# Four attention layers on one core: first row maxima in nine groups of six, normalisation on ScalarE in two layers, a projection dealt into attention's first phases

## The chip, the core and the metric

The kernel runs on one core of a Trainium2 chip. The metric is the device time in microseconds, the median of several runs. Before the change it is 5493.16 us (three runs, 5492.14 to 5493.9).

## What is computed

Four residual layers over x, 2048 tokens of 576 values in fp32: A, B, A, B. Each layer normalises x, projects it, does softmax attention with 32 heads of 18 values, projects the result back and adds it to x. In layers A every head has its own keys and values; in layers B all heads share one key and one value head.

```python
def _A_ref(x, wqkv, wo):                       # H = 32, Dh = 18
    q, k, v = split_heads(x @ wqkv)
    p = softmax(einsum("bhqd,bhkd->bhqk", q, k) * Dh ** -0.5)
    return merge(einsum("bhqk,bhkd->bhqd", p, v)) @ wo
...
x = x + _A_ref(layernorm(x), A_wqkv, A_wo)
x = x + _B_ref(layernorm(x), B_wq, B_wk, B_wv, B_wo)   # as A, one k and one v head for all
x = x + _A_ref(layernorm(x), A_wqkv, A_wo)
x = x + _B_ref(layernorm(x), B_wq, B_wk, B_wv, B_wo)
```

## The kernel before

**Number format.** Values that go through a projection are split into a high and a low part in TensorE's fp32r format; a projection of 512 tokens onto 128 columns is 14 matmuls (`TERMS`, line 32). Queries and keys stand in `big` with three rows for each value of a head (high, low, high against high, high, low), and two more rows that carry the negated row maximum, so that one matmul gives the score minus the maximum.

**A layer.** Layers are numbered 0 to 3; 0 and 2 are A (`is_a`), 1 and 3 are B. A layer has four stretches.

1. The previous layer's output projection (`out_proj`, `out_w`, lines 365 and 432), 16 chunks of 128 tokens. Between them the first chunks of x are normalised (`stats`, `scaled`, lines 301 and 313) and transposed by TensorE (`trans`, line 391). `stats` is VectorE and two small GpSimd instructions; `scaled` is two VectorE instructions.
2. The projections (loop at line 795), token block T of 512 by column tile t, with the transposes of the following chunks between them (`advance`, line 418). `project` (line 470) does the 14 matmuls into one PSUM bank, then evicts: high part by ScalarE (line 490), low part by VectorE (line 496) or, for a `filler`, by a second ScalarE copy and a GpSimd subtraction (lines 493 and 494). `store` sends the parts to a DRAM scratch, and `load_k` and `load_q` bring the rows of a head pair back into `big`. All these transfers are issued by SyncE, whose queue is in order. In layers B the order of t is 4, 0, 1, 2, 3; tile 4 holds the keys and values. In layers A values have projections of their own (`natural`, line 265, 14 matmuls of 288 columns).
3. A fill (lines 839 to 849 and 1024 to 1030): projections that the first head pair does not need.
4. Attention (lines 1038 to 1051): 16 head pairs by 4 blocks of 512 queries, 64 units of 32 exponentials (`exp_mm`, line 870: one score matmul and one ScalarE exponential of 128x512) and 32 maxima (`max_mm`, line 623: one score matmul and one VectorE reduction of 128x512). `UNIT` (lines 70 to 79) is the order, written by hand, of one unit in ten phases: e is an exponential, m a maximum, r a maximum whose block is first brought to SBUF by a ReLU on ScalarE (line 650) and then combined with its partner in one VectorE instruction (line 655), the digits are the head of the pair and the place in the list of banks. Each phase ends with so many columns of value matmuls (`pv_cols`), which lag 832 columns behind (`PV_LAG`), so that the first phase has none and the second none either.

**The first maxima.** The maxima run 56 ahead of the exponentials (`LEAD` = 14 steps of four). The first 56 are therefore put among the projections: `woven` (line 292) calls `max_pairs` (line 718), four maxima, after every so many matmuls that call `beat` (line 284). In layers A that is 8 calls 13 matmuls apart in the last value projections, then 6 calls 7 apart (lines 1025 and 1026); in layers B 5 calls 10 apart in block T = 2, 6 calls 6 or 7 apart in T = 3 and 3 in the fill (lines 804 to 807 and 1028). `max_place` and `m_first` (lines 592 and 611) say which query block and key block each is.

When all 32 maxima of a unit are there, `max_final` (line 851) reduces them, `max_store` (line 859) sends them to DRAM and `max_rows` (line 865) brings them back as rows of `big`; the exponentials of that unit wait for that. `todo` (line 968) holds such steps by the exponential at which they are due: `max_store`, `max_rows`, the loads of later pairs (`load_part`), the differences of keys for r (`diff_in` to `diff_rows`, lines 677 to 716), the output steps `o_mul` and `o_out` (lines 954 and 958).

**PSUM and spare buffers.** Seven banks are handed out oldest first (`bank`, `aged`, lines 158 to 164); a projection holds one until it ends. `relu` (line 966) is the list of buffers for the ReLU: one tile and, during attention, the chunk of x named in `AWAY` (line 65), which `x_away` (line 973) copies to DRAM at the start of attention and `x_back` returns near its end.

## Time and profile before

| what | value |
|---|---|
| median of three runs | 5493.16 us |
| profiled execution | 5495.69 us, span 5493.8 us |
| TensorE (PE) busy | 5479.3 us, 100%, 68190 matmuls |
| VectorE (DVE) busy | 4944.7 us, 90% |
| ScalarE (ACT) busy | 4810.0 us, 88% |
| GpSimd (POOL) busy | 1052.3 us, 19% |

PE is TensorE's matmuls and PEld its weight loads, which overlap them; DVE, ACT, POOL and SP are VectorE, ScalarE, GpSimd and SyncE, a q behind a name is that engine's queue. Matmuls are pipelined, so their durations overlap and the distance from start to start says what one costs. L877 is line 877 of the kernel before: the exponentials' score matmuls; L652 are the maxima's, L481 the projections, L275 the value projections, L927 the value matmuls; L882 is the exponential and L657 the maximum's reduction. In a row of the timeline the first number is the start in us of the span, the second the duration, and what stands in brackets is the engine's idle time before it and what ended it. xN says that the row merges N instructions.

### The profile page before, as it was taken

To read this page: it belongs to the slowest core of one execution; us is meant where nothing else is said; L and a number is where in the kernel's file an instruction comes from. 1 tells how busy PE (TensorE), PEld (TensorE's weight loads), DVE (VectorE), ACT (ScalarE), POOL (GpSimd) and SP (SyncE) were. 2 spreads that over 40 slices of the span, in tenths; PEclk is the share of its full clock that TensorE was granted. 3 is DMA by queue.
4 is the path that set the end of the run, shared out by engine and by line. 5 is a ranking of instruction groups with operands and counts; after the bars stand their busy time and mean duration, and the time that the engine had idled before them with its cause. 6 is when DMAs were issued, how large, how long until landed. Compare 5 with 4: busy or idle time off the path is not lost.

```text
span 5493.8 us, 166922 instructions
## 1 busy us (share of the span) xinstructions
PE 5479.3 (100%) x68190; PEld 3441.6 (63%) x68190; DVE 4944.7 (90%) x9741; ACT 4810.0 (88%) x9634; POOL 1052.3 (19%) x1614
## 2 busy tenths in 40 slices
PE   9999999999999999999999999999999999999999
PEld 8655555555855555555786555555558555555557
DVE  4799999998799999999637999999977999999995
ACT  3599999999289999999626999999992999999996
POOL 3121111212212111111211211111122121111111
PEclk9999999999999999999999999999999999999999
DMA  6321111111421110101253211111114111110102
GB/s 220 120 64 46 51 47 52 46 49 38 136 60 35 28 28 25 28 25 29 67 176 109 64 52 47 48 50 50 44 48 133 56 32 28 28 28 25 28 19 87
DMA packets 304321, 322.21 MB, mean 59 GB/s; under 512 B 130290, under 2 KB 239434, under 8 KB 294266
## 3 DMA queue, kind: packets, MB, share of 16 engines
...
## 4 chain that ended last, share of the span: by engine, by line
PE 97%; DMA 1%; DVE 1%; SPq 1%; POOL 0%; issue 0%; ACT 0%; POOLq 0%; ACTq 0%; DVEq 0%
PE oacc L927 38%; PE pse L877 23%; PE psm L652 21%; PE psn L275 7%; PE psq L481 6%; PE psm L639 2%; DVE mx L657 1%; PE ps L261 0%; POOL ev L494 0%; DMA m_d<-tr 0%; DMA big<-m_d 0%; DMA xx<-qk_d 0%; DMA rb<-r_d 0%; PE oacc L262 0%; SPq L553 0%
## 5 line engine op out<-in xcount | busy, mean ns | idle before, releaser
L882 ACT ACTIVATE pt<-pse 128x512 f32<-128x512 f32 x8192 | 4228.1, 613 | 62.1 <-PE psm L652 5.5
L657 DVE TENSOR_REDUCE mx<-psm 128x1 f32<-128x512 f32 x6208 | 3906.3, 683 | 113.0 <-PE psm L652 94.7
L652 PE MATMUL psm<-big 62*128 62x512 f32 x7200 | 2361.3, 438 | 1.9 <-ACT xo L650 1.1
L877 PE MATMUL pse<-big 64*128 64x512 f32 x8192 | 2358.5, 437 | 4.0 <-DMA big<-m_d 2.9
L927 PE MATMUL oacc<-pt,vbuf 128*19 128x256 f32 (+5 forms) x34864 | 1710.2, 319 | 0.1
L877 PEld LDWEIGHTS pse<-big 64*128 64x128 f32 x8192 | 1180.2, 184 | 478.8 <-ACT pt L882 167.0
L652 PEld LDWEIGHTS psm<-big 62*128 62x128 f32 x7200 | 1165.9, 184 | 445.9 <-ACT pt L882 342.1
L927 PEld LDWEIGHTS oacc<-pt,vbuf 128*19 128x19 f32 x34864 | 779.6, 98 | 733.2 <-issue 429.4
L943 POOL TENSOR_TENSOR rl<-lt,mone 128x8 f32<-128x8 f32 x256 | 419.6, 1639 | 1043.3 <-DMA lt<-os 1042.9
L927 PE MATMUL oacc<-pt,vy 128*19 128x256 f32 (+2 forms) x12272 | 570.5, 311 | 0.0
L186 POOL TENSOR_SCALAR hl<-neg 128x8 fp32r<-128x8 f32 x256 | 50.7, 198 | 2418.4 <-DVE neg L853 2418.4
L927 PEld LDWEIGHTS oacc<-pt,vy 128*19 128x19 f32 x12272 | 277.7, 98 | 250.7 <-issue 165.1
L490 ACT ACTIVATE ev<-psq 128x512 fp32r<-128x512 f32 (+1 forms) x112 | 66.9, 597 | 310.8 <-PE psq L481 224.3
L655 DVE CUSTOM_DVE_ANT_0 xo<-psm,xo 128x512 f32<-128x512 f32 x496 | 337.0, 679 | 0.8 <-PE psm L652 0.8
L655 DVE CUSTOM_DVE_ANT_0 relu<-psm,relu 128x512 f32<-128x512 f32 x496 | 337.2, 680 | 0.0
L650 ACT ACTIVATE xo<-psm 128x512 f32<-128x512 f32 x496 | 317.2, 640 | 1.5 <-DMA x_d<-xo 1.5
L275 PE MATMUL psn<-wsm,xx 128*128 128x288 f32 x2240 | 310.1, 297 | 0.0
L275 PEld LDWEIGHTS psn<-wsm,xx 128*128 128x128 f32 x2240 | 298.9, 188 | 12.1 <-issue 9.7
L650 ACT ACTIVATE relu<-psm 128x512 f32<-128x512 f32 x496 | 297.5, 600 | 0.0
L496 DVE TENSOR_TENSOR ev<-psq,ev 128x512 fp32r<-128x512 f32 (+1 forms) x84 | 57.9, 691 | 205.7 <-ACT ev L490 189.8
L956 POOL TENSOR_TENSOR os<-os,rb 128x256 f32<-128x256 f32 x256 | 188.1, 735 | 151.1 <-DMA rb<-r_d 96.6
L639 PE MATMUL psm<-big 54*128 54x512 f32 x512 | 204.9, 400 | 0.1
...
## 6 DMA issues: line engine op xcount, KB each, us to landing
...
rb<-r_d SPq DMA_DIRECT2D x512, 64.0 KB
...
o_d<-os SPq DMA_DIRECT2D x1024, 18.0 KB
...
big<-m_d SPq DMA_DIRECT2D x512, 4.0 KB
```

Source lines behind the costliest of these rows:

```text
L275: nc.tensor.matmul(ps, lhs[:, xc, :], wsm[:, wc, h * 288:(h + 1) * 288], start=i == 0, stop=i == len(TERMS) - 1)
L481: nc.tensor.matmul(ps[:n].rearrange("p (u t) -> p u t", u=2)[:, us], w[:, wc, :n], xts[T][:, us, xc, :], start=(xc, wc) == TERMS[0], stop= ...
L639: nc.tensor.matmul(ps.rearrange("p (h t) -> p h t", h=2) if p == 0 or not is_a else ps, q[b:b + 3 * DH, c0:c0 + P], k, start=True, stop=True)
L650: nc.scalar.activation(t, ps, AF.Relu)
L652: nc.tensor.matmul(ps, q[b:b + KM, c0:c0 + P], k[b:b + KM, kb * 512:(kb + 1) * 512], start=True, stop=True)
L655: nc.vector.tensor_tensor_reduce(t, ps, t, 1.0, LOWEST, OP.add, OP.max, mx[:, r:r + 1])
L657: nc.vector.reduce_max(mx[:, r:r + 1], ps, axis=AX.X)
L877: nc.tensor.matmul(e, k[r:r + KE, kc * P:(kc + 1) * P], q[r:r + KE, u * 512:(u + 1) * 512], start=True, stop=True)
L882: nc.scalar.activation(pt, e, AF.Exp, scale=SCALE)
L927: nc.tensor.matmul(oacc[j:j + DH + 1, c0:c1], v_of(kc)[:, 2 * p + a if is_a else 0, :], pts[tiles[a]][:, 256 * h + c0:256 * h + c1], start ...
L943: nc.gpsimd.tensor_tensor(rl, lts.pop((p, u)), mone, op=OP.pow)
L956: nc.gpsimd.tensor_tensor(t, t, rb, op=OP.mult)
```

## The change

- The first maxima are nine groups of six (`max_group`), called at written places (`A_AT`, `B_AT`) counted in matmuls: in layers A from ahead of the value projections on, in layers B from block T = 1 on; the last two are issued just before attention. `M_FIRST` says which they are. The first unit's `max_store` and `max_rows` and one load of queries are called at places too.
- In layers B `scaled` is two ScalarE instructions (Identity with scale and bias), for which `stats` gets a third GpSimd instruction; the evictions are of the filler kind from T = 1 on; the last block's keys and values are projected ahead of three of block 2's queries, and the transposes are drawn forward for that.
- The fill's last projection (column tile 3 of block 3) is not run in the fill. Its 14 matmuls are taken from a generator: up to eight ahead of the fifth operation of the first phase and the rest in the second, while it holds its bank; its eviction follows the last one.
- In layers A the last block's tile 4 comes before tile 0, and some loads move.
- Two chunks of x are away during attention instead of one (`AWAY`), so there are three buffers for the ReLU; they are copied away in block T = 3. There are three tiles for the later maxima instead of two. `o_mul` writes to the other half of its tile. The differences for the second pair start four steps later.

```diff
-AWAY = (15,)
+AWAY = (14, 15)
+A_AT = (88, 112, 126, 146, 166, 196, 220, 246, 268)
+B_AT = (28, 48, 68, 90, 106, 122, 142, 154, 178)
+M_FIRST = (((0, 0, 0, 4), (0, 1, 0, 4), (0, 2, 0, 4), (1, 0, 0, 3), (0, 3, 0, 4), (1, 0, 3, 4), (1, 1, 0, 4),
+            (1, 2, 0, 4), (1, 3, 0, 4)),
+           ((0, 0, 0, 4), (0, 1, 0, 4), (1, 0, 0, 4), (0, 2, 0, 4), (1, 1, 0, 2), (0, 3, 0, 4), (1, 1, 2, 4),
+            (1, 2, 0, 4), (1, 3, 0, 4)))
...
+LATE = 8
...
-    mx2 = [cst.tile([P, 32], F32, name=f"mx{i}") for i in range(2)]
+    mx2 = [cst.tile([P, 32], F32, name=f"mx{i}") for i in range(MX)]
...
+    def ranked(rank):
+        return [i for i in lru if i not in held][rank]
+
     def oldest(rank=0):
 
-        return lambda name: bank(lru[rank], name)
+        return lambda name: bank(ranked(rank), name)
...
-    weave = {"left": 0}
+    weave = {"n": 0, "at": []}
 
     def beat():
-        if weave["left"]:
-            weave["n"] += 1
-            if weave["n"] == weave["every"]:
-                weave["n"] = 0
-                weave["left"] -= 1
-                weave["f"]()
-
-    def woven(f, left, every):
-        assert not weave["left"]
-        weave.update(f=f, left=left, every=every, n=0)
+        weave["n"] += 1
+        while weave["at"] and weave["n"] >= weave["at"][0][0]:
+            weave["at"].pop(0)[1]()
+
+    def woven(*places):
+        assert not weave["at"]
+        weave.update(n=0, at=sorted(places, key=lambda x: x[0]))
...
-        rs = pool.tile([P, 2], F32, bufs=4, name="rs")
+        rs = pool.tile([P, 3], F32, bufs=4, name="rs")
...
         nc.gpsimd.tensor_tensor(rs[:, 1:2], rs[:, 0:1], mhalf, op=OP.pow)
+        if layer % 2:
+            nc.gpsimd.tensor_scalar(rs[:, 2:3], mv[:, 0:1], -1.0, rs[:, 1:2], op0=OP.mult, op1=OP.mult)
...
     def scaled(c, mv, rs):
         xc = xo[:, c, :]
         xh = pool.tile([P, 640], F32, tag="xh", bufs=2, name="xh")
-        nc.vector.tensor_scalar(xh[:, :D], xc, mv[:, 0:1], rs[:, 1:2], op0=OP.subtract, op1=OP.mult)
-        nc.vector.tensor_scalar(xh[:, D:], xc[:, 512:], mv[:, 0:1], rs[:, 1:2], op0=OP.subtract, op1=OP.mult)
+        if layer % 2:
+            nc.scalar.activation(xh[:, :D], xc, AF.Identity, bias=rs[:, 2:3], scale=rs[:, 1:2])
+            nc.scalar.activation(xh[:, D:], xc[:, 512:], AF.Identity, bias=rs[:, 2:3], scale=rs[:, 1:2])
+        else:
+            nc.vector.tensor_scalar(xh[:, :D], xc, mv[:, 0:1], rs[:, 1:2], op0=OP.subtract, op1=OP.mult)
+            nc.vector.tensor_scalar(xh[:, D:], xc[:, 512:], mv[:, 0:1], rs[:, 1:2], op0=OP.subtract, op1=OP.mult)
         return xh
...
-        def project(T, t, filler=False, half=None, terms=TERMS):
+        def project(*args, **kw):
+            for _ in project_parts(*args, **kw):
+                beat()
+
+        def project_parts(T, t, filler=False, half=None, terms=TERMS):
             t0 = T * 512
...
             for xc, wc in terms:
                 nc.tensor.matmul(ps[:n].rearrange("p (u t) -> p u t", u=2)[:, us], w[:, wc, :n], xts[T][:, us, xc, :],
                                  start=(xc, wc) == TERMS[0], stop=(xc, wc) == (TERMS if half != 0 else TERMS_LO)[-1])
-                beat()
+                yield
...
-        m_first = [] if is_a else ([(0, i // 2, i % 2) for i in range(8)] + [(1, i // 2, i % 2) for i in range(4)] +
...
+        m_first = [(u, i, kb) for u, kb, n, n1 in M_FIRST[layer % 2] for i in range(n, n1)]
...
-            if i < len(m_first):
+            if i < 32:
                 return (0, *m_first[i])
...
-                mxs[p, u] = pool.tile([P, 32], F32, name="mx") if (p, u) < (0, 2) else mx2[u % 2]
+                mxs[p, u] = pool.tile([P, 32], F32, name="mx") if (p, u) < (0, 2) else mx2[(4 * p + u) % MX]
...
-        def max_pairs():
-
-            if is_a:
-                if m_done[0] == 40:
-                    load_q(0, 1024, S)
-                run_todo(m_done[0] // 4)
-            elif m_done[0] == 44:
-                max_store(0, 0)
-            elif m_done[0] == 48:
-                max_rows(0, 0)
-            for i in range(4):
+        def max_group():
+            for i in range(6):
                 max_mm()
             while m_full:
                 max_final(*m_full.pop()[0])
...
+        def x_away():
+            for i, c in enumerate(AWAY):
+                nc.sync.dma_start(x_d[i], xo[:, c, :])
...
-        rest = [1, 2, 3, 5] if is_a else [2, 3]
+        rest = [1, 2, 5, 3] if is_a else [2, 3]
+        order = []
         for T in range(4):
-            if T == 0 and not is_a:
-                fixed_rows(k_slot(0), True)
-                fixed_rows(q_slot(0), False)
             if is_a:
-                ts = range(0 if T or layer else 3, 9) if T < 3 else (6, 7, 8, 0, 4)
+                ts = range(0 if T or layer else 3, 9) if T < 3 else (6, 7, 8, 4, 0)
             else:
                 ts = (4, 0, 1, 2, 3) if T < 3 else (4, 0, 1)
-            for i, t in enumerate(ts):
-                if not is_a and T == 2 and i == 1:
-                    woven(max_pairs, 5, 10)
-                elif not is_a and T == 3:
-                    woven(max_pairs, 2, (7, 6, 7)[i])
-                project(T, t, not is_a and T >= 2)
+            order += [(T, i, t) for i, t in enumerate(ts)]
+        if not is_a:
+            order.insert(12, order.pop(15))
+        for T, i, t in order:
+                if T == 0 and i == 0 and not is_a:
+                    fixed_rows(k_slot(0), True)
+                    fixed_rows(q_slot(0), False)
+                if not is_a and T == 1 and i == 0:
+                    woven(*((n, max_group) for n in B_AT), (B_AT[7] + 6, lambda: max_store(0, 0)),
+                          (B_AT[7] + 16, lambda: max_rows(0, 0)), (B_AT[7] + 26, lambda: load_q(0, 1536, S)))
+                project(T, t, not is_a and T >= 1)
                 if is_a and T == 3 and i == 2:
                     load_k(0, 0, 1536)
-                    load_q(0, 0, 512)
+                    load_q(0, 0, 1024)
+                    diff_rows(0)
+                    woven(*((n, max_group) for n in A_AT), (A_AT[6] + 4, lambda: max_store(0, 0)),
+                          (A_AT[6] + 18, lambda: max_rows(0, 0)), (A_AT[6] + 30, lambda: load_q(0, 1024, S)))
                     last_values()
+                if is_a and T == 3 and i == 4:
+                    load_k(0, 1536, S)
+                if T == 3 and i == (3 if is_a else 1):
+                    x_away()
 
                 for at_i, f in ((0, diff_in), (4 if is_a else 2, diff_split), (6 if is_a else 3, diff_out)):
                     if T == 2 and i == at_i:
                         f(0)
 
-                if T < 3 and ((i in (0, 1, 3, 5) if T + layer == 0 else i % 2) if is_a else i < 4):
-                    advance()
+                if T < 3 and ((i in (0, 1, 3, 5) if T + layer == 0 else i % 2) if is_a else i < (4, 5, 2)[T]):
+                    advance(2 if not is_a and T == 2 and i == 0 else 1)
                 if T == 0 and is_a and i < 6:
                     finish_loads()
                     if layer == 0 and i < 2:
@@ -826,16 +850,16 @@
                         load_wsm(i, A_wqkv[:, 2 * D:])
                     if layer == 0 and i < 3:
                         load_x(5 + i)
-                if not is_a and i < 2:
+                if not is_a and i < 2 and T * i < 3:
                     (load_q if i else load_k)(0, T * 512, T * 512 + 512)
-                if T == 3 and i == 2:
+                if not is_a and T == 3 and i == 2:
                     diff_rows(0)
                 if vts and i != 0:
                     v_trans(*vts.pop())
-            if is_a and T < 2:
-                for c in range(4 * T, 4 * T + 4):
-                    for h in range(2):
-                        nc.scalar.activation(v_dst(c)[:, h], project_v(c, h), AF.Copy)
+                if is_a and T < 2 and t == 8:
+                    for c in range(4 * T, 4 * T + 4):
+                        for h in range(2):
+                            nc.scalar.activation(v_dst(c)[:, h], project_v(c, h), AF.Copy)
         fill = []
         if is_a:
             for c in range(12, NCH):
@@ -844,10 +868,6 @@
         for t in rest:
             fill.append((project, (3, t, True)))
 
-        if is_a:
-            load_k(0, 1536, S)
-            load_q(0, 512, 1024)
...
             a, kc = (i // 2) % 2, i // 4 * 2 + i % 2
             q, k = ops(p)
-            by_act = reader[lru[rank]]
+            by_act = reader[ranked(rank)]
             e = oldest(rank)("pse")
...
         def o_mul(p, u):
-            t = sums[u % 2][:, :256]
-            nc.gpsimd.tensor_tensor(t, t, rb, op=OP.mult)
+            t = sums[u % 2]
+            nc.gpsimd.tensor_tensor(t[:, 256:], t[:, :256], rb, op=OP.mult)
 
         def o_out(p, u):
             for a in range(2):
                 c = (2 * p + a) * DH
                 for h in range(2):
                     j, t0 = 64 * a + 32 * h, u * 512 + 256 * h
-                    nc.sync.dma_start(o_d[c:c + DH, t0:t0 + 256], sums[u % 2][j:j + DH, :256])
+                    nc.sync.dma_start(o_d[c:c + DH, t0:t0 + 256], sums[u % 2][j:j + DH, 256:])
...
-        def x_away():
-            for i, c in enumerate(AWAY):
-                nc.sync.dma_start(x_d[i], xo[:, c, :])
-
         def x_back():
             for i, c in enumerate(AWAY):
                 nc.sync.dma_start(xo[:, c, :], x_d[i])
 
-        at(LEAD, x_away)
...
-                if is_a or p or u:
+                if p or u:
                     at(b + NM_AT, max_store, p, u)
                     at(b + (SOON[2] if b == ns - 1 else ROW_AT), max_rows, p, u)
...
                 for d, f in ((0, diff_in), (3, diff_split), (5, diff_out), (10 if p else 8, diff_rows)):
-                    at(max(LEAD, 32 * p - 8) + d, f, p + 1)
+                    at(max(LEAD + 4, 32 * p - 8) + d, f, p + 1)
...
+        late = project_parts(*fill.pop()[1])
         for i, (f, args) in enumerate(fill):
-            if is_a and i % 8 == 0:
-                woven(max_pairs, *((8, 13), (6, 7))[i // 8])
-            elif not is_a and i == 0:
-                woven(max_pairs, 3, 6)
             f(*args)
-        assert not weave["left"] and m_done[0] == 4 * LEAD
+        assert not weave["at"], weave
+        while m_done[0] < 4 * LEAD:
+            max_mm()
         e_next = [0, 0]
 
         def exp_next(a, rank=0, first=False):
@@ -1040,6 +1054,9 @@
             rows, cols = UNIT[phase % len(UNIT)]
             run_todo(LEAD + sum(e_next) / 4)
             for i, (kind, a, rank) in enumerate(rows):
+                if i == 4 and lagged < PV_LAG:
+                    for _ in range(LATE):
+                        next(late, None)
                 if kind == "e":
```

## Rows read from the trace of the kernel before

**Rows 1.** The page, busy time and share of the span of each engine.
```profile
PE 5479.3 (100%) x68190; PEld 3441.6 (63%) x68190; DVE 4944.7 (90%) x9741; ACT 4810.0 (88%) x9634; POOL 1052.3 (19%) x1614
```

**Rows 2.** Windows: PE, PEld, DVE, ACT, POOL busy, granted clock, DMA share, GB/s.
```profile
400.00:1340.00 940.00, 940.00 (x12767) 555.11 (x12755) 919.68 (x1802) 928.48 (x1853) 189.04 (x282) 1.00 0.17 46
1435.00:1475.00 40.00, 40.00 (x199) 32.27 (x198) 28.92 (x70) 12.63 (x28) 6.88 (x17) 1.00 0.58 191
1525.00:1535.00 10.00, 9.74 (x86) 4.93 (x83) 8.21 (x16) 8.32 (x17) 1.68 (x3) 0.83 0.75 237
```

**Rows 3.** Groups of instructions by line, 400 to 1340 us, the exponentials.
```profile
L882 ACT ACTIVATE pt<-pse 128x512 f32<-128x512 f32 x1648 | 851.5, 609 | 11.5
```

**Rows 4.** Timeline of PE in steady attention, layer 0.
```profile
1001.52 0.78 PE L877 MATMUL pse<-big 64*128 64x512 f32 x3
...
1002.31 0.90 PE L927 MATMUL oacc<-pt,vbuf 128*19 128x160 f32 x16
```

**Rows 5.** The chain of waits in layer 0: start, us, what.
```profile
146.32 14.83 PE psn L275 x112
...
172.50 1.92 PE psn L275 x13
175.08 1.93 PE psn L275 x13
```

**Rows 6.** Timeline of layer 1, projections and the start of attention.
```profile
1448.92 0.58 DVE L316 TENSOR_SCALAR xh<-xo,mv,rs 128x576 f32<-128x576 f32 x1
...
1482.11 1.66 PE L481 MATMUL psq<-yx,big 128*128 128x512 f32 x6 [0.47 <-DVE mx L657]
...
1487.47 1.34 PE L652 MATMUL psm<-big 62*128 62x512 f32 x4
...
1509.37 1.33 PE L652 MATMUL psm<-big 62*128 62x512 f32 x4
...
1512.46 0.73 PE L652 MATMUL psm<-big 62*128 62x512 f32 x4
...
1516.44 7.22 DVE L657 TENSOR_REDUCE mx<-psm 128x1 f32<-128x512 f32 x12
...
1516.97 1.27 PE L652 MATMUL psm<-big 62*128 62x512 f32 x4
...
1519.75 1.49 PE L652 MATMUL psm<-big 62*128 62x512 f32 x4
...
1524.37 0.47 PE L877 MATMUL pse<-big 64*128 64x512 f32 x1 [0.18 <-DMA big<-m_d]
...
1531.46 0.60 ACT L882 ACTIVATE pt<-pse 128x512 f32<-128x512 f32 x1 [1.53 <-PE psm L652]
```

**Rows 7.** Timeline of layer 0, last projection and the start of attention.
```profile
203.88 3.48 PE L481 MATMUL psq<-xx,big 128*128 128x512 f32 x14
...
207.29 0.50 PE L877 MATMUL pse<-big 64*128 64x512 f32 x1
...
207.63 0.40 PE L652 MATMUL psm<-big 62*128 62x512 f32 x2
...
207.86 0.39 PE L877 MATMUL pse<-big 64*128 64x512 f32 x1
...
208.43 4.53 ACT L882 ACTIVATE pt<-pse 128x512 f32<-128x512 f32 x9
...
212.05 0.95 PE L927 MATMUL oacc<-pt,vbuf 128*19 128x256 f32 x16
...
226.77 0.47 PE L877 MATMUL pse<-big 64*128 64x512 f32 x1 [0.57 <-DMA big<-m_d]
...
227.28 0.60 ACT L882 ACTIVATE pt<-pse 128x512 f32<-128x512 f32 x1 [0.89 <-PE psm L652]
```

**Rows 8.** Waits of ACT, 2940 to 3050 us, layer 2: total, times, longest.
```profile
ACT pt L882 <- PE psm L652: 1.6, 2, 0.9
```

**Rows 9.** Timeline of layer 3, the start of attention, ACT.
```profile
4272.22 0.60 ACT L650 ACTIVATE xo<-psm 128x512 f32<-128x512 f32 x1 [1.47 <-DMA x_d<-xo]
```

40 lines of the change are left out of this document (21 added, 19 removed).

## The prediction, made before the changed kernel was run

> **What bounds the kernel now.** The page comes first: TensorE is busy all the span, VectorE 90%, ScalarE 88% [rows 1]. A busy TensorE need not be full, so the windows come next: in a long stretch of layer 0's attention all three are nearly full (940.00, 919.68 and 928.48 of 940 us [rows 2]). That stretch holds 1648 exponentials [rows 3], so a unit of 32 exponentials and 32 maxima takes 940 × 32 / 1648 = 18.25 us. Which engine sets it shows in TensorE's own timeline: trains of score matmuls at 1001.52, then the value matmuls at 1002.31, each starting where the one before lets it, with no idle time noted [rows 4]. So attention is bound by TensorE, and the waits of ScalarE and VectorE follow it.
>
> Ahead of a layer's attention come the projections, with the first 56 maxima woven in. The chain of waits runs through TensorE there too: 112 value projections take 14.83 us, 0.132 each, and with four maxima after every 13 the period is 2.58 us (172.50 to 175.08) [rows 5]. 13 × 0.132 is 1.72, so a group of four maxima costs 0.86 us of TensorE. In layers 1 and 3 it is not full: several groups last 1.27 to 1.49 us where others take 0.73 [rows 6]. Then come the first phases: layer 0's first exponential matmul is at 207.29, the first value matmuls at 212.05, and between them ScalarE does nine exponentials in 4.53 us [rows 7]. There, and only there, TensorE has time left, because no value matmuls run for the first 832 columns.
>
> The sum is made on the profiled execution (5495.69 us around its span of 5493.8). The runs' median, 5493.16, is 2.5 us below; the same difference is taken off it. About 0.2%, 11 us, is what a measurement of this kernel can tell from no change.
>
> **The change part by part.**
>
> *Groups of six.* Fourteen groups of four become nine of six and two maxima that ride in the attention's first train. Six need one pair more than four. Pairs follow each other after 0.34 us (207.29 to 207.63) at the start of a train and after 0.23 (207.63 to 207.86) inside one [rows 7], so a group of six costs 0.86 + 0.23 = 1.09, at most 1.20. Before 14 × 0.86 = 12.0; after 9 × 1.09 + 0.23 = 10.0. That is -2.0 us a layer, -8.0 in all (-4 with 0.34 for the added pair).
>
> *The last projection.* Its 14 matmuls take 203.88 to 207.29, 3.41 us [rows 7], and leave the stretch ahead of attention. They come back as eight before the fifth operation of the first phase and six in the second, ahead of any value matmul. The blocks cost 3.41 plus one more way in and out, some 3.6 us. Around them stand 13 score matmuls of two phases and six of the third, ten pairs at 0.23 to 0.34: 2.3 to 3.4. Together 5.9 to 7.0 before the value matmuls, where it is 4.76 now: 1.2 to 2.2 longer. ScalarE also gets the block's two copies among the exponentials (0.6 each by the nearest row, an exponential), of which none may be hidden, and at worst all 3.6 is added. I take the middle of 1.2 and 3.6, 2.4. The move is worth -3.4 + 2.4 = -1.0 a layer, -4.0 in all. The 14 matmuls' result is written out by two more transfers on SyncE's queue in the first phases; their heads are not read before pair 10, and only the transfers behind them could feel it.
>
> *Waits ahead of attention in layers 1 and 3.* TensorE waits on VectorE for a free bank, or on the keys: groups of 1.34, 1.33, 1.27 and 1.49 instead of 0.73 are 0.61 + 0.60 + 0.54 + 0.76 = 2.5 us, a projection waits 0.47 and the first exponential 0.18, for the row of maxima [rows 6]: 3.2. I take 2.7 of it, as a wait of the 0.47 kind can stay. The maxima now begin one token block earlier, 20 or so matmuls apart, and the last block's keys are projected before three of the queries. Six maxima keep VectorE 6 × 0.60 = 3.6 us (12 in 7.22 [rows 6]). In the next 20 matmuls, some 4.6 us, TensorE has a transpose as well, and VectorE its parts of it; the move of the normalisation to ScalarE (0.58 us a chunk for the large piece [rows 6]) and of the evictions to ScalarE and GpSimd relieves VectorE, which is at 28.92 of 40 us in these projections while ScalarE is at 12.63 [rows 2]. So the added ScalarE work is costed at nothing, hidden by TensorE; were it not, each chunk would cost its 0.6. The same holds for a third small GpSimd instruction a chunk, with GpSimd at 6.88 of 40 [rows 2]. -2.7 a layer, -5.4 in all, none of it sure.
>
> *New waits there.* The last chunk's transposes now come right ahead of the projection that reads them: TensorE waits for ScalarE's copy, one instruction of 0.6 us. The row of maxima of the first unit is stored early enough, but its reload stands on SyncE's queue behind an eviction's store and two 288 KB copies of x; from there to the first exponential are 26 matmuls and a group, some 7 us, against 4.6 us (1519.75 to 1524.37) that store and reload take now. I take +0.6 + 0.5 = 1.1 a layer, +2.2 (0 to 6).
>
> *Starts of attention.* In layer 0 the second unit's row of maxima lands late: TensorE waits 0.57 and ScalarE 0.89 [rows 7]. Layer 2 has two such waits, 1.6 us [rows 8]. In layer 3 ScalarE waits 1.47 us to write into x's spare chunk, which is still being copied away [rows 9]. The change copies it away during the projections, and puts the second pair's differences four steps later, behind the second unit's store. I take 0.9 in layer 0, half of layer 2's 1.6 (one of its waits lies later), and 1.5 in layer 3: -3.2, none of it sure.
>
> *The clock.* Layer 1 has a wait of 1.53 at that place too [rows 6]. In the window 1525 to 1535 TensorE's granted clock was 0.83 on the mean [rows 2], so part of it at 1.2 instead of 2.4 GHz; ahead of it TensorE had been working, with no idle time in these rows beyond 0.18 and 0.47 us [rows 6]. The Trainium skill (TensorE: Matmul & The Clock Gate, "Why this matters for your kernels") puts such falls down to idle gaps between bursts of matmuls. The rows show no gap of note, so here the trace does not agree. By the page, the matmuls dealt into the first phases keep the clock up and all 1.5 us go; by the row, a fall may come anyway and none does. I take 0.7: -0.7.
>
> *The rest* is costed at nothing: the third spare buffer for the pre-maxima and the third tile of maxima act in steady attention, where TensorE is the bound; the product goes to the other half of its tile on GpSimd, which is at 19% [rows 1]; and more time between that and VectorE's next copy can only help. The second chunk of x comes back eight steps before the end, and is added to only at the output projection's fifteenth chunk.
>
> Sum: -8.0 - 4.0 - 5.4 + 2.2 - 3.2 - 0.7 = -19.1, so 5493.2 - 19.1 = **5474 us**.
>
> **The rivals.** *A transfer gates the first exponentials.* If the row of maxima, or the last keys, come as late in layers 1 and 3 as now, the 5.4 stay, and so may the 3.2 and the 0.7 at the starts: 5474 + 9.3 = 5483. For it speaks that SyncE's queue is in order and now takes x's copies before the reload; against it, 7 us of cover for 4.6.
>
> *The dealt projection is not hidden.* If the first phases grow by all 3.6 us, and six maxima in a row cost 1.20 a group, 1.2 × 4 and 4 come back: 5474 + 8.8 = 5483. For it: TensorE needs nearly all of these 4.76 us once two switches are added. Against: ScalarE's 4.53 us for nine exponentials runs beside.
>
> *The change misses: VectorE becomes the bound ahead of attention in layers 1 and 3.* Six maxima need 3.6 us, a chunk's transpose and statistics some 2 us more; in the next 20 matmuls, 4.6 us, with a group (1.1) and a transpose (0.9) that is 5.6 of 6.6, so VectorE is short only where two chunks fall into one such stretch, by about 1 us, in perhaps three places a layer: 5474 + 6 = 5480.
>
> *Slower: steady attention loses its pattern.* Four pre-maxima a unit now turn over three buffers, so the choice of the exponential's buffers, which follows who read what last, no longer repeats from unit to unit. A matmul that gets one more wait costs what a broken train costs, 0.34 - 0.23 = 0.11 us. Once a unit in 252 units is 28 us: 5474 + 28 = 5502; it decides from 0.08 a unit, where the 19 are gone. Against it: ScalarE and VectorE show slack in the window [rows 2], and TensorE's trains show no idle time [rows 4].
>
> **How the numbers follow.** The forecast's own case gets 0.58, the three mild rivals together 0.32, the slower one 0.10. Over 0.2% faster is below 5482: 0.56 of the first case and 0.10 of the mild ones, 0.66; same 0.26, of which 0.02 is the first case's and 0.02 a lesser form of the slower one; slower 0.08. Low end: the late projection at 1.2 instead of 2.4 (-4.8), no new waits (-2.2), the whole of the clock and of layer 2's waits (-1.6), and as much again in steady attention if the third buffer spares a wait somewhere: 5461. High end: past the mild rivals at 5483, to where two of them meet, 5491.
>
> **What would show it.** Right: in layers 0 and 2 the stretch from the last value projections to the first exponential shrinks by about 5.4 us, in layers 1 and 3 by some 7; the time from there to the first value matmuls grows from 4.8 to about 7; groups of six last some 1.1 us from start to start of what stands around them; ScalarE's waits of 0.9 to 1.5 us at the starts are gone; and a unit of steady attention stays at 18.25 us. Wrong: a unit of another length, as 0.04 us there are 10 us in all; a first value matmul over 8.4 us after the first exponential; waits of TensorE on VectorE around the groups; or a reload of the maxima landing after the last projection.

## The result and the profile after the change

The changed kernel takes 5519.16 us (median of four runs, 5518.48 to 5523.91), the kernel before 5492.93 beside it: the ratio is 1.005, with an interval of 1.0032 to 1.0067. The change makes the kernel 26 us slower; 5474 had been forecast, with a range up to 5491. The profiled execution is the slowest of the four, 5523.91 us around a span of 5522.1, against 5495.69 around 5493.8 before.

The page's first part and a window of steady attention, to be laid beside [rows 1, 2], and the exponentials of that window beside [rows 3]:

```profile
PE 5480.8 (99%) x68190; PEld 3451.3 (63%) x68190; DVE 4918.1 (89%) x9667; ACT 4850.5 (88%) x9708; POOL 1077.8 (20%) x1657
```

```profile
400.00:1340.00 940.00, 940.00 (x12772) 555.61 (x12772) 919.58 (x1802) 928.76 (x1855) 186.39 (x279) 1.00 0.17 47
```

```profile
L902 ACT ACTIVATE pt<-pse 128x512 f32<-128x512 f32 x1649 | 851.6, 609 | 11.2
```

TensorE has the same 68190 matmuls and 1.5 us more busy time, but the span is 28.3 us longer: TensorE stands idle for 41 us of it, where it was 14.5 before [rows 1]. Steady attention has not changed: 1649 exponentials in 940 us where there were 1648. (L902 is the exponential now, L671 and L658 the maxima, L897 the exponentials' score matmuls, L500 the projections, L287 the value projections, L947 the value matmuls, L273 and L274 the transposes.)

So the loss lies at the two ends of each layer. The table is worked out from the starts and ends of the exponentials in both traces: *front* is the time from the last exponential of the layer before (in layer 0 from the start) to the first of this layer; the first, second and third unit are 32 exponentials each, from start to start; then the last 128 exponentials, to their end. It is after less before, in us.

| layer | front | first unit | second and third | last 128 |
|---|---|---|---|---|
| 0 | +3.8 | +4.1 | +4.8 | +0.9 |
| 1 | -2.6 | +5.0 | 0.0 | +0.5 |
| 2 | +0.6 | +4.5 | +3.8 | +0.8 |
| 3 | -1.2 | +5.0 | 0.0 | +0.5 |
| sum | +0.5 | +18.6 | +8.7 | +2.6 |

Together 30.4 us; the units between and the end of the kernel give 2.1 back, which makes the 28.3 by which the spans differ. The fronts, from which 24.8 us were to go, gave nothing. Four views show the waits. The timeline of TensorE in layer 0, where the value projections begin:

```profile
151.77 5.85 PE L287 MATMUL psn<-wsm,yx 128*128 128x288 f32 x43
161.29 0.47 PE L671 MATMUL psm<-big 62*128 62x512 f32 x1 [3.67 <-DMA big<-qk_d]
162.38 1.62 PE L671 MATMUL psm<-big 62*128 62x512 f32 x5 [0.63 <-DMA big<-qk_d]
163.93 5.73 PE L287 MATMUL psn<-wsm,yx 128*128 128x288 f32 x24
```

and the window behind that wait (columns as in [rows 2], the granted clock third from the end):

```profile
162.00:169.00 7.00, 6.62 (x26) 5.93 (x27) 3.57 (x6) 0.41 (x1) 0.00 (x0) 0.52 0.01 2
```

The first group of six comes 88 matmuls after the keys' loads were issued, and the loads have not landed: TensorE waits 3.67 and 0.63 us. Behind the wait the granted clock is 0.52, so 1.2 instead of 2.4 GHz nearly throughout: 24 value matmuls take 5.73 us, where at 0.132 each [rows 5] they would take 3.17.

The same engine at the start of layer 0's third unit, and SyncE's queue ahead of it (start, us, what):

```profile
256.24 0.47 PE L897 MATMUL pse<-big 64*128 64x512 f32 x1 [2.90 <-DMA big<-m_d]
```

```profile
243.35 3.29 SPq L707 DMA_DIRECT2D xx<-qk_d x4
246.74 0.57 SPq L883 DMA_DIRECT2D m_d<-tr x1
...
247.99 2.57 SPq L735 DMA_DIRECT2D xx<-kd_d x2
...
251.70 0.52 SPq L887 DMA_DIRECT2D big<-m_d x2
```

The third unit's row of maxima (store 246.74, reload 251.70) now stands between the differences' transfers, which hold the queue for 3.29 and 2.57 us. TensorE waits 2.90 us.

Layer 1, block 2, where two chunks' transposes now come in a row:

```profile
1494.59 0.60 PE L273 MATMUL ps<-ident,xh 128*128 128x128 f32 x4
...
1495.13 0.60 PE L273 MATMUL ps<-ident,xh 128*128 128x128 f32 x4
1498.21 0.33 PE L274 MATMUL oacc<-ident,xh 128*128 128x128 f32 x1 [2.48 <-DVE xx L268]
```

The fifth transpose of a chunk goes to `oacc`, one bank for all chunks, and the second chunk's waits 2.48 us until VectorE has read the first's.

And layer 1's first phases, TensorE and ScalarE:

```profile
1535.64 0.50 PE L671 MATMUL psm<-big 62*128 62x512 f32 x2 [0.56 <-ACT evr L512]
1536.08 2.11 PE L500 MATMUL psq<-xx,big 128*128 128x512 f32 x8
...
1539.81 0.50 PE L671 MATMUL psm<-big 62*128 62x512 f32 x1 [0.73 <-ACT pt L902]
1540.24 1.66 PE L500 MATMUL psq<-xx,big 128*128 128x512 f32 x6
...
1543.13 0.50 PE L658 MATMUL psm<-big 54*128 54x512 f32 x1 [0.33 <-ACT evr L512]
...
1544.06 0.95 PE L947 MATMUL oacc<-pt,vbuf 128*19 128x256 f32 x16
```

```profile
1535.48 0.60 ACT L902 ACTIVATE pt<-pse 128x512 f32<-128x512 f32 x1
1538.68 2.06 ACT L902 ACTIVATE pt<-pse 128x512 f32<-128x512 f32 x4 [2.60 <-PE pse L897]
1542.00 0.60 ACT L509 ACTIVATE ev<-psq 128x512 fp32r<-128x512 f32 x1 [1.26 <-PE psq L500]
```

The dealt matmuls (L500, 8 and 6) stand in TensorE's queue when ScalarE has been given one exponential: it is idle for 2.60 us behind the first block and 1.26 behind the second, and then TensorE waits 0.73 for ScalarE. So no exponential runs beside the blocks. The first value matmuls come 8.58 us after the first exponential, where it was 3.62 to 4.01 in the trace before; "over 8.4" was one of the prediction's signs of being wrong.

One more wait is new in layers 1 and 3, ahead of the second unit: its row of maxima is late (the same timeline of TensorE, layer 1; in layer 3 it is 1.09).

```profile
1559.43 0.47 PE L897 MATMUL pse<-big 64*128 64x512 f32 x1 [1.28 <-DMA big<-m_d]
```

### The profile page after: what moved, and what is told of

The parts are those of the page before. It is cut to its first block, busy times and chain, and to the rows that moved or that the text cites. A ratio compares the mean times of both kernels' runs of the same rounds, so it can differ in the third digit from the quotient of the medians.

```text
span 5522.1 us, 166476 instructions
## 1 busy us (share of the span) xinstructions
PE 5480.8 (99%) x68190; PEld 3451.3 (63%) x68190; DVE 4918.1 (89%) x9667; ACT 4850.5 (88%) x9708; POOL 1077.8 (20%) x1657
## 4 chain that ended last, share of the span: by engine, by line
PE 96%; DMA 1%; DVE 1%; issue 0%; SPq 0%; ACT 0%; POOL 0%; ACTq 0%; POOLq 0%; DVEq 0%
PE oacc L947 38%; PE pse L897 23%; PE psm L671 21%; PE psn L287 6%; PE psq L500 6%; PE psm L658 2%; DVE mx L676 1%; DMA m_d<-tr 0%; PE ps L273 0%; DMA big<-qk_d 0%; DMA big<-m_d 0%; POOL ev L513 0%; ACT evr L512 0%; PE oacc L274 0%; DVE yx L267 0%
## 5 line engine op out<-in xcount | busy, mean ns | idle before, releaser
L902 ACT ACTIVATE pt<-pse 128x512 f32<-128x512 f32 x8192 | 4226.4, 611 | 82.0 <-PE pse L897 15.3
L671 PE MATMUL psm<-big 62*128 62x512 f32 x7200 | 2360.5, 438 | 13.1 <-DMA big<-qk_d 7.8
L897 PE MATMUL pse<-big 64*128 64x512 f32 x8192 | 2355.2, 437 | 8.5 <-DMA big<-m_d 8.5
L947 PE MATMUL oacc<-pt,vbuf 128*19 128x256 f32 (+5 forms) x34864 | 1709.4, 319 | 0.4 <-DVE os L198 0.3
L897 PEld LDWEIGHTS pse<-big 64*128 64x128 f32 x8192 | 1180.6, 184 | 482.3 <-ACT pt L902 174.3
L671 PEld LDWEIGHTS psm<-big 62*128 62x128 f32 x7200 | 1169.4, 184 | 456.3 <-ACT pt L902 346.4
L947 PEld LDWEIGHTS oacc<-pt,vbuf 128*19 128x19 f32 x34864 | 779.2, 98 | 731.7 <-issue 426.5
L947 PE MATMUL oacc<-pt,vy 128*19 128x256 f32 (+2 forms) x12272 | 572.1, 312 | 0.0
L674 DVE CUSTOM_DVE_ANT_0 xo<-psm,xo 128x512 f32<-128x512 f32 x664 | 452.2, 681 | 0.0
L947 PEld LDWEIGHTS oacc<-pt,vy 128*19 128x19 f32 x12272 | 278.2, 98 | 251.2 <-issue 165.8
L669 ACT ACTIVATE xo<-psm 128x512 f32<-128x512 f32 x664 | 409.6, 617 | 0.0
L287 PE MATMUL psn<-wsm,xx 128*128 128x288 f32 x2240 | 308.7, 297 | 0.0
L287 PEld LDWEIGHTS psn<-wsm,xx 128*128 128x128 f32 x2240 | 298.8, 188 | 9.9 <-issue 7.2
L674 DVE CUSTOM_DVE_ANT_0 relu<-psm,relu 128x512 f32<-128x512 f32 x328 | 223.4, 681 | 0.0
L658 PE MATMUL psm<-big 54*128 54x512 f32 x512 | 203.5, 397 | 1.2 <-ACT evr L512 1.2
L669 ACT ACTIVATE relu<-psm 128x512 f32<-128x512 f32 x328 | 202.2, 616 | 0.0
```

The source lines that it names most:

```text
L287: nc.tensor.matmul(ps, lhs[:, xc, :], wsm[:, wc, h * 288:(h + 1) * 288], start=i == 0, stop=i == len(TERMS) - 1)
L658: nc.tensor.matmul(ps.rearrange("p (h t) -> p h t", h=2) if p == 0 or not is_a else ps, q[b:b + 3 * DH, c0:c0 + P], k, start=True, stop=True)
L669: nc.scalar.activation(t, ps, AF.Relu)
L671: nc.tensor.matmul(ps, q[b:b + KM, c0:c0 + P], k[b:b + KM, kb * 512:(kb + 1) * 512], start=True, stop=True)
L674: nc.vector.tensor_tensor_reduce(t, ps, t, 1.0, LOWEST, OP.add, OP.max, mx[:, r:r + 1])
L897: nc.tensor.matmul(e, k[r:r + KE, kc * P:(kc + 1) * P], q[r:r + KE, u * 512:(u + 1) * 512], start=True, stop=True)
```

## The experiments

All times are medians, against the kernel before on the same chip (5493.28 for the first four, 5493.18 for the next four, 5492.62 for the three after them, 5491.61 for the last). Fronts, units and the first value matmul are worked out as for the table above.

### The dealing undone

```diff
-        late = project_parts(*fill.pop()[1])
+        late = iter(())
```

> The changed kernel with its last projection run in the fill again, nothing dealt into the first phases. Theory A, four separate causes: the dealt projection lengthens a layer's first unit by 4.9 us (22.98 against 18.0 without waits in layer 0) and saves 3.4 ahead of it, so this run gains 1.5 us a layer: 5519 - 6 = 5513 us, first units of 18 to 19.5 us, and TensorE's wait of 2.9 us at 253 us stays. Theory B, one cause: the transfers of the dealt projection on SyncE's queue also delay the rows of maxima, so the waits at 253 and 1558 us go too, with the clock's fall after the first: some 18 us, 5501.

Measured: 5520.3 us (ratio 1.0048, 1.0025 to 1.0071), as slow as the change. The fronts become 1.9, 3.1, 4.1 and 3.4 us longer, 12.5 together, and the stages from the first to the last exponential 3.3, 4.1, 2.1 and 4.2 shorter, 13.7 together. The dealing moves the matmuls and hides none. The first value matmul comes 5.13 to 5.19 us after the first exponential, so 3.4 of the 8.58 were the dealt block, its whole length; 1.2 to 1.6 above before are still there, from the two last maxima and the waits around them. The wait of 1.28 us ahead of layer 1's second unit and that of 1.09 in layer 3 are gone.

The dealing has a gain as well, which is in these sums: without it the clock falls at the start of attention in all four layers. The windows of the first 10 us from layer 1's first exponential, in the change and in this run, have a granted clock of 1.00 and 0.83:

```profile
1535.48:1545.48 10.00, 8.78 (x51) 5.09 (x53) 6.53 (x12) 6.15 (x14) 2.92 (x4) 1.00 0.57 213
```

```profile
1537.17:1547.17 10.00, 9.04 (x75) 4.57 (x79) 8.78 (x18) 8.07 (x17) 1.69 (x3) 0.83 0.72 227
```

In the same windows of layers 0, 2 and 3 it is 1.00 in the change and 0.83, 0.66 and 0.83 here. What these four windows lack of 1.00 is 8.5 us of clock, an estimate of what the falls cost at most.

### The second pair's differences at their old place

```diff
-                    at(max(LEAD + 4, 32 * p - 8) + d, f, p + 1)
+                    at(max(LEAD, 32 * p - 8) + d, f, p + 1)
```

> The changed kernel with the second pair's key differences four steps earlier again, as before the change. Theory A: they crowd SyncE's queue ahead of the third unit's row of maxima, so the wait of 2.9 us at 253 and at 3004 us and the clock's fall after it go, second units of 18.3 instead of 21.6 and third ones of 18.3 instead of 19.8: 4.7 us a layer in layers 0 and 2, 5510 us; a wait of under 1 us for the second unit's row may come back, as before the change. Theory B: the dealt projection's transfers delay it, the wait stays above 2 us, 5517 to 5520.

Measured: 5518.1 us (1.0044, 1.0024 to 1.0064). The second and third units of layers 0 and 2 last 18.23 to 18.26 us again, so the wait of 2.90 and the clock behind it come from the shift of four steps. (How much it costs differs: in the seven profiled runs that have the shift, these four units together are 5.7 to 9.7 us longer than here.) But the first unit of layer 0 grows from 22.98 to 26.39, of layer 2 from 23.19 to 24.14. The timeline of TensorE in layer 0's first phases says why:

```profile
214.81 0.73 PE L500 MATMUL psq<-xx,big 128*128 128x512 f32 x2
215.72 1.07 PE L500 MATMUL psq<-xx,big 128*128 128x512 f32 x2 [0.18 <-DMA xx<-qk_d]
217.09 1.22 PE L500 MATMUL psq<-xx,big 128*128 128x512 f32 x2 [0.30 <-DMA xx<-qk_d]
```

The differences' loads write into `xx`, which the dealt projection still reads (in this run a part of column tile 3 of block 3 is computed from the differences in place of x, in layers 0 and 2). The shift is thus no part of its own: it is the price of the dealing.

### The first groups of the A layers later

```diff
-A_AT = (88, 112, 126, 146, 166, 196, 220, 246, 268)
+A_AT = (124, 138, 158, 178, 198, 218, 238, 256, 276)
```

> The changed kernel with the nine groups of layers A at 124, 138, 158, 178, 198, 218, 238, 256 and 276 matmuls instead of 88 to 268. Theory A: the first group waits for the first pair's rows, 3.7 + 0.6 us of idle TensorE, and the clock falls to 1.2 GHz for 6.8 us; starting at 124, all that goes in layers 0 and 2: 2 x 7 = 14 us, 5505 us. Rival: VectorE is the bound with groups of six closer together, the stretch to the first exponential gets 2 us shorter at most: 5515.

Measured: 5507.75 us (1.0025, 1.0014 to 1.0036). This one edit gives 11 us back. The front of layer 0 falls from 212.20 to 202.74, that of layer 2 from 256.95 to 250.71; the groups wait for nothing (TensorE's timeline in layer 0):

```profile
162.85 0.97 PE L671 MATMUL psm<-big 62*128 62x512 f32 x6
...
172.44 2.92 PE L287 MATMUL psn<-wsm,xx 128*128 128x288 f32 x20
175.29 0.96 PE L671 MATMUL psm<-big 62*128 62x512 f32 x6
176.19 2.93 PE L287 MATMUL psn<-wsm,xx 128*128 128x288 f32 x20
```

From 172.44 to 176.19 are 3.75 us; less 20 value matmuls of 0.132 this leaves 1.11 for a group of six, and the next three periods leave 1.10 to 1.39; the prediction, counting the same way, had 1.09, at most 1.20. The two fronts are 5.7 and 5.6 us shorter than before the change, and 5.4 had been forecast for each (in layer 0, 1.0 of the 5.7 stands ahead of the value projections).

### A bank of its own for chunk 14's transpose

```diff
-layer == 0 and c in (1, 3, 7))
+layer == 0 and c in (1, 3, 7) or layer % 2 == 1 and c == 14)
```

> The changed kernel with a bank of its own for the fifth transpose of chunk 14 in layers B, so that two chunks' transposes in a row do not share the one accumulator bank. Theory A: TensorE's wait of 2.48 us at 1495.7 and 4248.2 us goes, and layer 3's fall of the clock after it (1.7 us): 2 x 2.5 + 1.7 = 6.7, 5512 us. Rival: the same split by VectorE holds up the next projection instead, which needs it: 2 us at most, 5517.

Measured: 5522.35 us (1.0053, 1.003 to 1.0076). The 2.48 becomes 0.55, and that wait moves into the next group (the timeline of TensorE, layer 1):

```profile
1499.21 0.83 PE L671 MATMUL psm<-big 62*128 62x512 f32 x2 [0.55 <-DVE xx L267]
1499.97 3.35 PE L500 MATMUL psq<-yx,big 128*128 128x512 f32 x8
```

Eight matmuls take 3.35 us there, where the eight dealt ones above took 2.11: the clock has fallen here too. Layer 1's front stays (148.26 for 148.14), layer 3's is 1.6 shorter.

### All four edits

> The four edits together: last projection run in the fill again, second pair's differences back at their old place, groups of the A layers placed behind the landing of their keys, a bank of their own for chunk 14's transposes in the B layers. Theory (four separate losses, which add): front of layer 0 about 205.5, of layer 2 about 254, of layers 1 and 3 about 151; first units 19.5 to 20 in all layers, second units 18.3; no clock fall ahead of attention in layers 0 and 2; total 5493 +- 4, as before, since the groups of six and the earlier copies of x then give back little more than what B's front keeps losing. Rival (the losses share one cause, the early end of the front, so each repair only moves the wait): the rows of maxima are late again in layers 0 and 2, 5502 or more.

Measured: 5495.42 us (1.0005, 0.9996 to 1.0015): as before the change. Fronts 205.81, 151.17, 253.89, 151.54; second units 18.25 to 18.26; first units 20.55, 20.09, 19.18, 21.89. Made one by one the edits give back 8 us in all (-1, 1, 11 and -3), together 24. The runs above show one reason: the dealing and the shift belong to each other, so undoing one leaves the other's price.

### Transposes one by one, the groups moved to suit

```diff
-B_AT = (28, 48, 68, 90, 106, 122, 142, 154, 178)
+B_AT = (28, 48, 68, 90, 106, 122, 156, 170, 184)
...
-            order.insert(12, order.pop(15))
+            order.insert(13, order.pop(15))
...
-i < (4, 5, 2)[T])
-                    advance(2 if not is_a and T == 2 and i == 0 else 1)
+i < (4, 5, 3)[T])
+                    advance()
```

> As the run with all four edits, but in the B layers chunk 14's and 15's transposes come one after each of two projections instead of both in a row, the last block's keys are projected one place later, and the last three groups and the row's store and reload 14 matmuls later. Theory (two chunks in a row on one shared bank are what costs there): no TensorE wait over 0.7 us on the split at that place, no clock fall in layers 1 and 3, fronts of layers 1 and 3 at most 149.5 (before 150.8 and 150.6), total 3 us under the run with all four edits. Rival (the row of maxima, now later, becomes the last thing): a wait for it of 1 us or more at the first exponential, total not under that run.

Measured: 5505.87 us (1.0024, 1.0014 to 1.0034), 10 more than the run with all four edits. A miss: the wait on the shared bank is gone, but in layers 1 and 3 a group now stands ahead of its keys. TensorE's timeline in layer 1:

```profile
1493.41 0.47 PE L671 MATMUL psm<-big 62*128 62x512 f32 x1 [2.72 <-DMA big<-qk_d]
1494.32 1.61 PE L671 MATMUL psm<-big 62*128 62x512 f32 x5 [0.44 <-DMA big<-qk_d]
```

The fronts are 159.20 and 157.99, 8 and 6.5 longer. All waits for keys come to 4.6 and 3.6 us in these two fronts, and the group's five matmuls of 1.61 us show the lower clock behind the first.

### VectorE normalises again in layers 1 and 3

```diff
-        if layer % 2:
+        if False:
             nc.scalar.activation(xh[:, :D], xc, AF.Identity, bias=rs[:, 2:3], scale=rs[:, 1:2])
```

> The change with one part undone: layers 1 and 3 normalise on VectorE again. Theory (the move to ScalarE is hidden both ways): fronts of layers 1 and 3 within 0.5 us of the change's 148.14 and 149.34, total within 3 us of the change. Rival (VectorE is what those fronts wait for): TensorE's waits for the bank that VectorE reads grow, by 0.6 to 1 us in each of some four places a layer, fronts 2.5 us or more longer, total 5 us or more above the change.

Measured: 5529.23 us (1.0064, 1.0047 to 1.0081), 10 above the change: the rival holds. The transposes of layer 1 that follow a group, first in this run, then in the change:

```profile
1472.17 0.66 PE L273 MATMUL ps<-ident,xh 128*128 128x128 f32 x4 [1.33 <-DVE mx L676]
...
1490.17 0.66 PE L273 MATMUL ps<-ident,xh 128*128 128x128 f32 x4 [1.25 <-DVE mx L676]
```

```profile
1475.57 0.66 PE L273 MATMUL ps<-ident,xh 128*128 128x128 f32 x4 [0.69 <-DVE mx L676]
...
1490.66 0.66 PE L273 MATMUL ps<-ident,xh 128*128 128x128 f32 x4 [0.60 <-DVE mx L676]
```

Each wait is twice as long without ScalarE, and the fronts of layers 1 and 3 grow by 4.8 and 1.9 us. So the ScalarE part of the change is a gain.

### The dealt projection's low part evicted by VectorE

```diff
-            fill.append((project, (3, t, True)))
+            fill.append((project, (3, t, t != 3)))
```

> The change with one edit: the dealt projection's low part is evicted by one VectorE instruction instead of a second ScalarE copy and a GpSimd subtraction. Theory (ScalarE is the bound of the first phases, so its two copies lie on the path): the first unit shrinks by some 0.5 us in each layer, the first value matmul comes some 0.5 us earlier than 8.58, total -2 to -3 against the change. Rival (TensorE is the bound there and the copies are hidden): first units unchanged within 0.1.

Measured: 5517.63 us (1.0044, 1.0029 to 1.0059). The first value matmul comes at 8.39 to 8.45 instead of 8.58 and the first units change by -0.5 to +0.4 with no pattern. Where TensorE waited 0.33 us in layer 1 for ScalarE's second copy, it waits 0.58 for VectorE's subtraction.

So the copies cost little; the block itself is what costs.

### The oldest free bank in the last loop

```diff
-exp_next(int(e_next[0] > e_next[1]), next(i for i, j in enumerate(lru) if j not in held))
+exp_next(int(e_next[0] > e_next[1]), 0)
```

> The change with one edit: in the last loop of a layer's attention the exponential takes the oldest free bank. (The helper that ranks the banks now leaves out held ones itself, and this loop still skips them too, so that it takes a younger one.) Theory: that double skip is why the last 128 exponentials of a layer last 69.7 to 70.1 us after the change and 69.2 before; with the edit 69.2 again in all four layers, 2.4 us in all. Rival (the second chunk of x that comes back there delays them): unchanged at 69.7 to 70.1.

Measured: 5520.66 us (1.0051, 1.0033 to 1.007; two runs, too few for 2 us). The last 128 exponentials last 69.54, 69.23, 69.22 and 69.25 us, against 70.09, 69.72, 70.03 and 69.72 in the change and 69.22 to 69.26 before. ScalarE's timeline at the end of layer 1, first in the change, then in this run:

```profile
2703.00 3.54 ACT L902 ACTIVATE pt<-pse 128x512 f32<-128x512 f32 x7 [0.61 <-PE pse L897]
```

```profile
2696.74 9.19 ACT L902 ACTIVATE pt<-pse 128x512 f32<-128x512 f32 x18
```

The 0.61 is gone. `ranked` leaves out held banks, and its caller in the last loop, whose line is not in the diff, still skips them too. That costs 2.3 us over the four layers.

### A version put together: groups of six in A, of four in B

Against the run with all four edits: layers B have the order, the transposes and the fourteen groups of before, but keep ScalarE's normalisation, the evictions and the early copies of x; the last two maxima stand at a place of their own; the last loop takes the oldest bank.

```diff
+(290, lambda: max_group(2))
...
-            order.insert(12, order.pop(15))
...
-woven(*((n, max_group) for n in B_AT), ...
+woven(*((n, lambda: max_group(4)) for n in (10, 20, 30, 40, 50, 63, 70, 76, 82, 91, 98, 104, 110, 116)),
+      (100, lambda: max_store(0, 0)), (111, lambda: max_rows(0, 0)))
```

> A version put together from the parts that held: layers A with groups of six behind the landing of their keys and the last two maxima at a place of their own ahead of the last projection, layers B with the order, the transposes and the groups of four of before, but normalised on ScalarE; no dealing, differences at their old place, oldest free bank in the last loop, x copied away early. Theory (the parts are independent, those of B that lose are its new order and its paired transposes): fronts of layers 0 and 2 about 205.8 and 253.9, of layers 1 and 3 about 149; first units at most 19; last 128 exponentials 69.2; total 5484 to 5487, under before. Rival (what is saved in the front comes back as a clock fall or a late row at the start of attention): first units over 19.5 with a clock at 1.2 GHz there, total 5490 to 5496.

Measured: 5485.43 us (0.9989, 0.998 to 0.9998), faster than both kernels. Fronts 208.17, 150.15, 254.50, 149.74; first value matmuls 3.63 to 4.12 after the first exponential; first units 19.40, 19.88, 18.22, 18.78. TensorE's timeline at the start of layer 1's attention, and a window around it:

```profile
1524.25 0.47 PE L897 MATMUL pse<-big 64*128 64x512 f32 x1 [1.08 <-DMA big<-m_d]
```

```profile
1517.00:1532.00 15.00, 13.79 (x62) 8.16 (x62) 11.87 (x21) 7.78 (x16) 2.95 (x4) 0.79 0.65 213
```

### The same with groups of six in B

```diff
+woven(*((n, max_group) for n in (14, 28, 42, 54, 66, 74, 84, 93, 104)), (114, lambda: max_group(2)),
+      (98, lambda: max_store(0, 0)), (109, lambda: max_rows(0, 0)))
```

> As the version put together, but layers B with nine groups of six and one of two, at places from block 2 on. Theory (a group of six costs 1.1 us and spares 2 us a layer wherever its keys have landed and VectorE keeps up): fronts of layers 1 and 3 1.5 to 2 us shorter than with groups of four, total 3 to 4 us less. Rival (six maxima in a row make TensorE wait for VectorE in layers B): waits on VectorE of 0.5 us and more around the groups, fronts not shorter.

Measured: 5498.09 us (1.0009, 1.0 to 1.0018), 13 more than with groups of four. The fronts of layers 1 and 3 are 3.9 and 5.8 us longer; the wait is for keys more than for VectorE (0.70 to 0.87 at two places a layer). TensorE's timeline in layer 1:

```profile
1509.54 0.47 PE L671 MATMUL psm<-big 62*128 62x512 f32 x1 [2.44 <-DMA big<-qk_d]
```

### x copied away behind the row of maxima

```diff
-                          (100, lambda: max_store(0, 0)), (111, lambda: max_rows(0, 0)))
+                          (100, lambda: max_store(0, 0)), (111, lambda: max_rows(0, 0)), (113, x_away))
```

> The version put together (groups of four in layers B), with one edit: in layers B the two chunks of x are copied away behind the reload of the first row of maxima on SyncE's queue, not ahead of its store. Theory (the two copies of 288 KB hold up the row's store and reload): the waits of 1.08 and 0.92 us for the row ahead of the first exponentials of layers 1 and 3 go, with them the clock at 1.2 GHz there; fronts of layers 1 and 3 149.1 and 148.8, first unit of layer 1 at most 19, total 5481 to 5483. Rival (the row is late by itself, or the copies are then late for the first ReLU in x): the waits stay at 0.5 us or more, or a wait of ScalarE for the copy comes in the first unit; total 5485 or more.

Measured: 5485.25 us (0.9989, 0.998 to 0.9998), the same as the version above. The rows are as the theory has them: fronts 149.04 and 148.86, first units 18.18 and 17.90, and in the same stretch of TensorE's timeline and the same window

```profile
1522.02 0.47 PE L897 MATMUL pse<-big 64*128 64x512 f32 x1
```

```profile
1517.00:1532.00 15.00, 14.55 (x112) 8.40 (x110) 14.18 (x28) 11.00 (x23) 2.96 (x4) 1.00 0.63 204
```

no wait and a granted clock of 1.00 for 0.79. But the median did not follow: the profile of the version above was its slowest execution (5490.17, of 5483.62 to 5490.17), and the mean granted clock rounds to 1.000 in five of its eleven runs and in nine of the eleven here: the falls differ from execution to execution. The gain of moving the copies stays below what can be told.

## Why the prediction was wrong

The terms of the sum against what the traces show, in us over the four layers:

| where | forecast | measured |
|---|---|---|
| fronts of layers 0 and 2 | -10.8 | +4.4 |
| fronts of layers 1 and 3 | -14.0 | -3.9 |
| first units | +5.7 | +18.6 |
| second and third units | 0 | +8.7 |
| last 128 exponentials | 0 | +2.6 |
| rest | 0 | -2.1 |
| sum | -19.1 | +28.3 |

(The forecast's fronts are the groups, the dealt projection taken out, and in layers 1 and 3 the waits; its first units are the dealing's 9.6 less 0.7 of clock, layer 3's 1.5, and the 0.9 and 0.8 for the late rows of layers 0 and 2, whose waits end where the second unit starts.)

**Groups of six: priced by their length, placed for nothing.** In layers 0 and 2 the price was about right: 1.10 to 1.39 us a group against 1.09 in the run with the groups later, and there the fronts fall by what was forecast. But the step took the place as free. The change starts the groups 36 matmuls earlier than that run, ahead of their keys' landing, and the wait of 4.3 us in layer 0 and 3.1 in layer 2, with the clock behind it, is 9.5 and 6.2 us of front (0.7 of the 9.5 stands ahead of the value projections); the run that only moves the groups gives them back. The trace before had no such wait because its first group came later, so it held no row that named it. What could have been read there are SyncE's queue and TensorE's timeline, layer 0:

```profile
152.09 0.86 SPq L559 DMA_DIRECT2D big<-qk_d x2
...
155.40 2.11 SPq L716 DMA_DIRECT2D big<-kd_d x2
```

```profile
169.18 0.73 PE L652 MATMUL psm<-big 62*128 62x512 f32 x4
```

The loads were issued from 152.09 to 155.40 us, the DMA engines moved data until some 161.5, and the first maxima came at 169.18. The change issues the loads at the same time (151.75) and its first group stands at 157.62, where the wait of 3.67 begins.

**The dealt projection: the wrong one of two figures, and a rider.** 2.4 was taken between 1.2 and 3.6. The run without the dealing shows 3.4 from the first exponential to the first value matmul, the block's whole length; the rival "not hidden" was right in its mechanism. The reason given for hiding it, that nine exponentials run beside, fails because the block comes when one has been issued: ScalarE idles 2.60 and 1.26 us. And the dealing forces the differences later (they write what it reads), which the sum counted as part of a *gain* of 0.9 + 0.8 at the starts; it costs 9.7 in the second and third units, which the run with the differences at their old place gives back. Of these 9.7, 7.6 still stand in the run without the dealing. By these figures the dealing as a whole loses some 9 us: 13.7 - 12.5 + 7.6.

The prediction also priced its two more transfers on SyncE's queue at nothing. In all seven traces with the dealing the second unit's row of maxima is late in layers 1 and 3, by 0.50 to 2.15 us of TensorE's time; in the seven without (the one before included) no such wait is over 0.45. In layer 1 the row's reload is issued 6.9 us behind its store in the change, and 2.0 in the run without the dealing. That it is these transfers that hold it up is likely and not shown by itself.

**Two maxima in attention's first train.** Costed at 0.23 us a layer. With the waits of 0.56 and 0.69 around them they move the first value matmul from 3.6 to 4.0 to 5.1 to 5.2; in the version where they have a place ahead of the last projection it is 3.63 to 4.12.

**Waits ahead of attention in layers 1 and 3.** The forecast took 2.7 of 3.2 us a layer away and added 1.1. Most of the 2.7 stayed. In layer 1, besides the waits of 0.69 and 0.60 shown above, two groups last 1.35 and 1.32 us where the others take 0.96 to 1.03, and one projection waits (TensorE's timeline in the change):

```profile
1506.57 1.35 PE L671 MATMUL psm<-big 62*128 62x512 f32 x6
...
1517.96 1.32 PE L671 MATMUL psm<-big 62*128 62x512 f32 x6
...
1523.45 5.76 PE L500 MATMUL psq<-xx,big 128*128 128x512 f32 x24 [0.31 <-DVE mx L676]
```

Counted as the prediction counted [rows 6], with 0.97 for a group, that is 0.69 + 0.60 + 0.38 + 0.35 + 0.31 = 2.3 us; before it was 3.0 without the wait for the row. So 0.7 went, and the rival in which VectorE stays the bound there was partly right. Without ScalarE's share the waits of 0.69 and 0.60 would have been twice as long, so that part of the step holds. The wait of 0.77 for ScalarE's copy ahead of the last keys came as foreseen (0.6); the row of maxima made none at the first exponential, where 0.5 had been added. Missed was the second chunk in a row on the one shared bank, 2.48 us, the largest wait there: the prediction counted the transposes' matmuls and not the bank that the fifth of them goes to. Repairing it alone did not pay, since part of it moved to the next group.

These pieces nearly make up layer 1's front: -3.4 for the dealt projection, -2.0 for the groups, -0.7, +0.8 and +2.5 are -2.8, and -2.6 was measured. The -2.0 is the forecast's own figure here; no run shows it in layers 1 and 3, and with the order of before groups of six were 3.9 and 5.8 us slower there than groups of four.

**The last loop** was costed at nothing, with attention as bound by TensorE; in it a younger bank for the exponentials cost 2.3 us.

**The clock.** Put at -0.7 us for one fall that would go, as the dealt matmuls might keep the clock up. It went, and the runs bear the reason out: in the first 10 us of a layer's attention the seven traces with the dealing show a fall in 1 of 28 starts, the seven without it (the one before included) in 17 of 28. But other falls came ahead of attention and in it: behind the waits of 3.67 and 2.75 us for the keys in layers 0 and 2, of 2.90 for the rows, and in layer 3 of 2.48 for the bank. The Trainium skill (TensorE: Matmul & The Clock Gate, "Why this matters for your kernels") puts such falls down to idle gaps between bursts of matmuls, and behind these waits the trace agrees, where the prediction had set it aside for the trace of before. The gaps do not settle it alone: the same 2.48 us in layer 1 was followed by a fall in the run with the groups later and by none in the change, and the version put together shows a fall at 211.5 us with no wait of TensorE over 0.34 us in the 15 us ahead of it. The run with x's copies behind the row has neither the wait nor the fall. In these traces a new wait ahead of attention cost about twice its length: the 4.3 and 3.1 us for the keys stand beside 9.5 and 6.2 us of front, and 4.6 and 3.6 us in the run with the transposes one by one beside 8 and 6.5.

**What held:** steady attention with three ReLU buffers and three tiles of maxima kept its unit (on the mean of a layer's units from the fourth on, 18.26 to 18.29 before and 18.25 to 18.28 after), so the rival on the slower side was wrong, and the loss came by none of the rivals' ways alone. Apart from the 0.77 us for ScalarE's copy, TensorE waits for no ScalarE or GpSimd instruction in the fronts of layers 1 and 3.

**What stays open:** how much of the loss each clock fall carries. The records put TensorE at 1.2 GHz for some 27 us of the change's span and for 3.4 of the span before, the last microseconds left aside; at half the clock that is at most some 12 of the 28.3 us, an estimate. The falls come in some executions and not in others, so the pieces above are from one profiled execution each and need not add up to the medians.
